# Key tiles fetched half by half, one half per step, in a windowed-attention and MoE kernel

## The chip, the cores and the metric

The kernel runs on one core of a Trainium2 chip. The metric is the device time of one execution in microseconds (us). The profile is one further execution, recorded by the hardware profiler. Engines are called as in the profile: PE (matrix multiplication) with PEld (its weight loads), DVE (vector), ACT (activations), POOL (GpSimd) and SP (a queue that issues transfers). POOL issues transfers too: all loads of this kernel's inputs after the first ones go through it[...].

## What is computed

Attention over a window of 32 tokens to both sides for 8 batches of 8 heads, 576 tokens each, head size 64, and on its output a two-layer network for 4608 tokens (512 to 2048 to 512):

```python
def _attn_ref(q, k, v):
    scores = scale * np.matmul(q, k.transpose(0, 1, 3, 2))
    mask = np.abs(pos[:, None] - pos[None, :]) <= 32
    scores = np.where(mask, scores, -1000000000.0)
    attn = np.exp(scores - np.max(scores, axis=-1, keepdims=True))
    attn = attn / (np.sum(attn, axis=-1, keepdims=True) + 1e-09)
    return np.matmul(attn, v)

def _moe_ref(x, w_in, w_out):
    h = x @ w_in
    g = h * (1.0 / (1.0 + np.exp(-1.702 * h)))
    return g @ w_out
```

The inputs q, k and v have the shape (8, 8, 576, 64); the output is (4608, 512) in float32.

## The kernel before

The 4608 tokens of all batches form one line. It is cut into 36 blocks of 128 tokens (index u, or m for V) and into tiles of 512 tokens (index i) for the loading of keys and queries. The whole order is written by hand: `head()` runs first, then `window(w)` for w = 4 to 19. Such a window is called a step here. Each engine works through its own instructions in the order in which the code names them, and waits where data or a buffer isn't ready.

A step w from 5 to 17 does three things at once. The attention of blocks a = 2w and b = 2w + 1 is computed: `scores`, `band` (the mask), `values`, `norm`. The first layer of the network runs for the pair of blocks of step w-1 (`layer1(w - 1, d)`, eight calls, list l1), the second layer for that of step w-2 (`product`, L394, with sums on DVE in `g_sums`, `keep` and `result`). PE therefore executes in a step: scores, products 1, 2, 5 and 6, the first call of layer1, the values, and then products and layer1 in turn.

The output of `norm`, x, must be transposed for layer1. From block 10 on a transfer does that: `x_T` (L315) issues a transposing transfer on SP for each block, xT<-x. Layer1 of the next step waits for both of the pair.

Keys and queries go through two stages. POOL loads them into a staging tile (ks and qs, three buffers each), and SP transposes them from there:

- `load_keys(i)` (L141 to L146) loads the keys of tile i in four chunks of 128 tokens, one transfer each, two where a chunk crosses from one batch to the next. `load_heads(i, "q")` (L138) loads the queries, in one or two transfers.
- `keys_X(i, c)` (L151) transposes chunk c into kT, a ring of 1536 tokens. `queries_X(i)` (L221) transposes a tile's queries into qT, after `pair_heads` has arranged them on DVE (qc<-qs).
- `load_v(m)` (L157) loads V for block m into one of 8 buffers; the transfer waits until `values` of block m-8 has read that buffer. `odd_v` copies V to a second layout.

Inside a step, the local function `loads()` (L606) issues V for blocks 2w + 6 and 2w + 7, then, in the even steps up to w = 10, the keys and queries of a whole tile, and in w = 4 those of two tiles. `loads()` stands at the front of the step, so on POOL the loads of a step follow directly on those of the step before; in w = 4 they stand behind two copies on POOL that wait for transposes of tile 3.

Towards the end of the step `feed(w)` (L727) prepares what later steps need: with i = (w + 4) // 2, an odd step pairs and transposes the queries of tile i and its key chunks 2 and 3, an even step transposes its chunks 0 and 1. SP takes these behind the xT transposes of the same step and ahead of those of the next.

Of the kernel before, what the change touches and what calls it, by code (L numbers as in the profile page):

```python
# [16 lines left out]
BF16 = mybir.dt.bfloat16  # L17
# [5 lines left out]
JT = 4  # L23
# [5 lines left out]
class _Kernel:  # L29
# [108 lines left out]
            self.nc.gpsimd.dma_start(self.stage[key][off // JT:(off + m) // JT, lo:hi, :],  # L138
                                     src[b, lo:hi, s:s + m, :].rearrange("h (p j) d -> p h (j d)", j=JT))

    def load_keys(self, i):  # L141

        kn = self.stage["k", i] = self.work.tile([128, JT, self.H, self.D], BF16, name="ks", tag="ks", bufs=3)
        for c in range(JT):
            for off, b, s, n in self.pieces(512 * i + 128 * c, 128):
                self.nc.gpsimd.dma_start(kn[off:off + n, c], self.k[b, :, s:s + n, :].rearrange("h s d -> s h d"))  # L146

# [447 lines left out]
    def window(self, w):  # L595
        nc, dve, sp = self.nc, self.nc.vector, self.nc.sync
        a, b = 2 * w, 2 * w + 1
        att = w < self.NW
        t, act = w - 2, nc.scalar
        l1 = [(lambda d=d: self.layer1(w - 1, d)) for d in range(8)] if w <= self.NW else []  # L600

        def run(lst, n=1):
            for _ in range(min(n, len(lst))):
                lst.pop(0)()

        def loads():  # L606
            for m in (2 * w + 6, 2 * w + 7):
                if m < self.NU:
                    self.load_v(m)
            for i in ((4, 5) if w == 4 else (w // 2 + 3,) if w % 2 == 0 else ()):  # L610
                if 512 * i < self.N:
                    self.load_keys(i)
                    self.load_heads(i, "q")

        if w == 4:
            l2 = [(lambda u=u, i=i: self.layer2(u, i, "oh"[u % 2], (dve, act)[u % 2])) for u in (4, 5) for i in range(4)]
            self.scores(7)
            self.scores(a)
            run(l2, 3)
            self.band(7)  # L620
            self.scores(b)
            run(l2)
            self.band(a)
            self.values(7, "th")
            self.gelu_table()
            for hp in range(4):
                self.pair_heads("q", 3, hp, act)
            self.queries_X(3)
            self.nc.gpsimd.tensor_copy(self.kT[:, :, RING:], self.kT[:, :, 0:64])
            self.nc.gpsimd.tensor_copy(self.qT[:, :, RP:RP + 8], self.qT[:, :, 0:8])  # L630
            loads()
            self.band(b)
            self.norm(7)
            run(l2, 2)
            self.values(a)
            self.values(b)
            run(l2)
            self.x_T(7, "t", nc.scalar)
            self.norm(a)
            self.x_T(a)  # L640
            self.norm(b)
            self.x_T(b)
            run(l2)
            for m in (10, 11):
                self.odd_v(m, dve)
            run(l1, 8)
            self.g_sums(w - 1, 0)
            self.feed(w)
            return
        loads()  # L650
        if not att:
            self.close(w, l1)
            return
        self.scores(a)
        if w > 5:
            self.scores(b)
        self.g_sums(t, 1, (0, 1))
        self.product(t, 1, "o")
        self.keep(t, 1, dve)
        self.product(t, 2, "h")  # L660
        if w == 5:
            self.scores(b)
        self.g_sums(t, 1, (2, 3))
        self.result(t, 11)
        self.gelu_table()
        self.product(t, 5, "t")
        self.band(a)
        self.product(t, 6)
        self.band(b, 0)
        self.keep(t, 6, dve)  # L670
        self.band(b, 1)
        run(l1)
        self.values(a)
        self.values(b)
        self.norm(a)
        self.x_T(a)
        self.product(t, 7)
        self.keep(t, 7, dve)
        self.result(t, 22)
        run(l1, 1)  # L680
        self.product(t, 4)
        self.result(t, 21, act)
        self.norm(b)
        self.x_T(b)
        self.product(t, 3)
        self.result(t, 12)
        run(l1, len(l1) - 4)
        self.g_sums(w - 1, 0)
        self.feed(w)
        run(l1, 4)  # L690
# [109 lines left out]
```

## Time and profile before

| what | value |
| --- | --- |
| median of 11 runs | 304.66 us |
| lowest, highest | 301.29 us, 309.97 us |
| the profiled execution | 310.95 us |
| its span, first to last instruction | 309.2 us |
| mean granted TensorE clock | 0.971 |
| data moved | 38.81 MB in 126026 packets |
| POOL's transfer queue (q0) | 79008 packets, 18.16 MB |
| SP's transfer queue (q1) | 46528 packets, 19.67 MB |

The profiled execution is slower than most of the runs. The rows of the profile name an operation by its line, its engine and "output<-input", a count, its busy time, the mean duration of one, and after the second bar the idle time of its engine just ahead of it with what ended that time. In the slices each digit is the busy share of one fortieth of the span (7.73 us), in tenths. A transfer has two times: that of its issue on the engine that owns the queue, and that from the start of the issue to its landing. xT<-x takes 2.4 us to landing at least, 4.2 in the median and 11.6 at most; ks<-in_k_dram 2.4, 8.1 and 21.7 us.

### The profile page before, as it was taken

To read this page: it belongs to the slowest core of one execution; us is meant where nothing else is said; L and a number is where in the kernel's file an instruction comes from. 1 tells how busy PE (TensorE), PEld (TensorE's weight loads), DVE (VectorE), ACT (ScalarE), POOL (GpSimd) and SP (SyncE) were. 2 spreads that over 40 slices of the span, in tenths; PEclk is the share of its full clock that TensorE was granted. 3 is DMA by queue.
4 is the path that set the end of the run, shared out by engine and by line. 5 is a ranking of instruction groups with operands and counts; after the bars stand their busy time and mean duration, and the time that the engine had idled before them with its cause. 6 is when DMAs were issued, how large, how long until landed. Compare 5 with 4: busy or idle time off the path is not lost.

```text
span 309.2 us, 9525 instructions
## 1 busy us (share of the span) xinstructions
PE 292.0 (94%) x4020; PEld 237.9 (77%) x4020; DVE 192.1 (62%) x571; ACT 187.6 (61%) x310; POOL 89.9 (29%) x132
## 2 busy tenths in 40 slices
PE   7889999999998499999589999999999999999995
PEld 3468765857886388888458888888888888888884
DVE  3653557776658148696535857776685858684353
ACT  4675457797848039485716766758584849485330
POOL 8784517830784322352043202020200000000000
PEclk9979999999999689999959999999999999999999
DMA  9999996999999999999989994895755030303012
GB/s 144 159 206 204 194 190 127 173 144 159 126 155 146 165 130 175 123 178 141 145 103 157 181 178 36 118 135 125 89 115 125 19 105 0 105 4 102 2 68 68
DMA packets 126026, 38.81 MB, mean 126 GB/s; under 512 B 104481, under 2 KB 121633, under 8 KB 125985
## 3 DMA queue, kind: packets, MB, share of 16 engines
q0 software_dynamic: 79008, 18.16, 72.6%
q1 hardware_dynamic: 46528, 19.67, 36.7%
q8 instruction: 31, 0.51, 0.7%
q10 hardware_dynamic: 448, 0.39, 0.5%
q14 instruction: 11, 0.08, 0.1%
HBM read 36.96 MB, written 9.44 MB: 150 GB/s over the span
## 4 chain that ended last, share of the span: by engine, by line
PE 84%; DMA 10%; POOL 2%; DVE 1%; ACT 1%; issue 0%; POOLq 0%; DVEq 0%
PE h_ps L332 40%; PE o_ps L394 28%; DMA xT<-x 7%; PE o_ps L344 7%; PE pv L292 4%; PE sc L263 3%; DMA qs<-in_q_dram 3%; PE tp L176 1%; POOL ve L157 1%; PE tp L319 0%; ACT g L334 0%; POOL ks L138 0%; DVE qc L106 0%; DVE o_sb L412 0%; POOL neg L237 0%
## 5 line engine op out<-in xcount | busy, mean ns | idle before, releaser
L332 PE MATMUL h_ps<-xT,w_in_sb 128*128 128x256 bf16 x1152 | 138.8, 277 | 10.3 <-DMA xT<-x 10.3
L334 ACT ACTIVATE g<-h_ps 128x512 f16<-128x512 f32 x144 | 85.7, 596 | 90.0 <-PE h_ps L332 88.7
L332 PEld LDWEIGHTS <-w_in_sb 128*128 128x128 bf16 x1152 | 113.7, 99 | 25.9 <-issue 5.8
L157 POOL DMA_DIRECT2D ve<-in_v_dram x40 | 34.0, 854 | 88.4 <-PE pv L292 68.3
L394 PEld LDWEIGHTS <-gs 128*128 128x128 f16 x480 | 46.5, 99 | 6.5
L394 PE MATMUL o_ps<-w_sum,gs 128*128 128x256 f16 x360 | 46.0, 279 | 0.0
L269 ACT ACTIVATE p<-sc 128x512 bf16<-128x512 f32 x72 | 37.2, 604 | 2.8 <-PE sc L263 2.6
L394 PEld LDWEIGHTS <-g 128*128 128x128 f16 x360 | 34.1, 98 | 4.5 <-ACT g L334 0.2
L371 DVE TENSOR_TENSOR gs<-g 128x512 f16<-128x512 f16 x30 | 12.7, 422 | 35.7 <-ACT g L334 35.7
L304 DVE TENSOR_TENSOR x<-pv,rec 128x256 bf16<-128x256 f32 x72 | 30.5, 424 | 2.5
L394 PE MATMUL o_ps<-w_out_sb,g 128*128 128x256 f16 x240 | 29.0, 273 | 0.0
L106 DVE COPY part<-o_ps 128x256 f32<-128x256 f32 x45 | 19.0, 423 | 14.1 <-PE o_ps L394 12.9
L303 DVE RECIPROCAL rec<-pv 128x4 f32<-128x4 f32 x72 | 12.5, 174 | 23.8 <-PE pv L292 23.8
L412 DVE TENSOR_TENSOR o_sb<-o_ps,part 128x256 f32<-128x256 f32 x45 | 19.0, 422 | 13.1 <-PE o_ps L394 12.5
L146 POOL DMA_DIRECT2D ks<-in_k_dram x27 | 22.7, 871 | 10.1 <-DMA qs<-in_q_dram 3.7
L281 DVE TENSOR_TENSOR p<-p,mask 128x512 bf16<-128x512 bf16 x64 | 24.8, 423 | 1.3 <-ACT p L269 1.1
L344 PE MATMUL o_ps<-w_out_sb,g 128*128 128x512 f16 x96 | 23.2, 380 | 0.0
L106 DVE COPY vo<-ve 64x528 bf16<-64x528 bf16 x65 | 21.1, 325 | 1.9 <-DMA ve<-in_v_dram 0.4
L431 ACT ACT_TABLE_LOAD x15 | 19.2, 1283 | 0.3
L269 ACT ACT_TABLE_LOAD x15 | 19.2, 1283 | 0.3
L292 PEld LDWEIGHTS <-p 128*64 128x64 bf16 x576 | 12.1, 117 | 6.8 <-DVE p L281 2.5
L394 PE MATMUL o_ps<-w_out_sb,gs 128*128 128x256 f16 x120 | 15.6, 273 | 0.0
(72 smaller groups left out, 247.3 us busy)
## 6 DMA issues: line engine op xcount, KB each, us to landing
out_dram<-o_sb SPq DMA_DIRECT2D x34, 256.0 KB, 3.1
ve<-in_v_dram POOLq DMA_DIRECT2D x32, 128.0 KB, 6.2
ks<-in_k_dram POOLq DMA_DIRECT2D x22, 128.0 KB, 8.2
w_in_sb<-in_moe_w_in_dram POOLq DMA_DIRECT2D x4, 512.0 KB, 11.5
w_out_sb<-in_moe_w_out_dram POOLq DMA_DIRECT2D x4, 512.0 KB, 12.1
qs<-in_q_dram POOLq DMA_DIRECT2D x2, 448.0 KB, 14.2
qs<-in_q_dram POOLq DMA_DIRECT2D x3, 256.0 KB, 7.7
qs<-in_q_dram POOLq DMA_DIRECT2D x2, 384.0 KB, 14.9
```

The costliest lines, as they stand in the source:

```text
L106: (eng.copy if eng is self.nc.scalar else eng.tensor_copy)(out, in_)
L146: self.nc.gpsimd.dma_start(kn[off:off + n, c], self.k[b, :, s:s + n, :].rearrange("h s d -> s h d"))
L157: self.nc.gpsimd.dma_start(self.ve[m % NV][off:off + n, :, :self.D], self.v[b, :, s:s + n, :].rearrange("h s d -> s h d"))
L269: nc.scalar.activation(p[:, eo].rearrange("k h (s j) -> k h s j", j=JT), sc[eo].rearrange("k h (j s) -> k h s j", j=JT), AF.Exp, scale=sel ...
L281: self.nc.vector.tensor_mul(pv, pv, msk.to_broadcast([128, 4, 2, SQ]))
L292: nc.tensor.matmul(acc[half][blk * 64:blk * 64 + 64, hh, :], p[:, h % 2, h // 2 * 2 + blk, :], vt[:, h, :D + 1], start=(hh == 0), stop=(hh ...
L304: nc.vector.tensor_mul(x[:, hs, :], acc[half][:, :, :D], rec[:, hs, :].to_broadcast([128, 4, D]))
L332: nc.tensor.matmul(hps[:, i, :], self.w_in_sb[:, kr, ff * 128:(ff + 1) * 128], self.xT[t][:, kr, :], start=(i == 0 and kr == 0), stop=(i = ...
L334: nc.scalar.activation(self.g[t][:, ffs[0]:ffs[1] + 1:ffs[1] - ffs[0], :], hps, AF.Gelu_apprx_sigmoid)
L344: nc.tensor.matmul(o_ps, self.g[t][:, ff, s * 128:(s + 1) * 128], self.w_out_sb[:, ff, :], start=(ff == 0), stop=(ff == self.NFF - 1))
L394: nc.tensor.matmul(self.part[t, key], x, y, start=(first and k == 0), stop=(k == 7), skip_group_check=True)
L431: self.nc.scalar.activation(self.spark, self.spark, AF.Gelu_apprx_sigmoid)
```

## The change

The keys of a tile after the fourth are no longer loaded at once. In an odd step w the first two chunks of tile (w + 5) // 2 are loaded, in the following even step the last two and the tile's queries. Tile 4 is loaded whole in w = 4, as before. Tile 5, which was loaded in w = 4 as well, is loaded in w = 5 and 6; tile 6 in 7 and 8 where it was in 6; tile 7 in 9 and 10 where it was in 8; tile 8 in 11 and 12 where it was in 10. `load_keys` takes a list of chunks and makes the staging tile at its first call for a tile. Nothing else is touched: V still comes first in each step, and `feed` keeps its order.

```diff
-    def load_keys(self, i):
-
-        kn = self.stage["k", i] = self.work.tile([128, JT, self.H, self.D], BF16, name="ks", tag="ks", bufs=3)
-        for c in range(JT):
+    def load_keys(self, i, chunks=range(JT)):
+
+        if ("k", i) not in self.stage:
+            self.stage["k", i] = self.work.tile([128, JT, self.H, self.D], BF16, name="ks", tag="ks", bufs=3)
+        kn = self.stage["k", i]
+        for c in chunks:
             for off, b, s, n in self.pieces(512 * i + 128 * c, 128):
                 self.nc.gpsimd.dma_start(kn[off:off + n, c], self.k[b, :, s:s + n, :].rearrange("h s d -> s h d"))
...
-            for i in ((4, 5) if w == 4 else (w // 2 + 3,) if w % 2 == 0 else ()):
-                if 512 * i < self.N:
-                    self.load_keys(i)
+            i = (w + 5) // 2
+            if 512 * i < self.N:
+                self.load_keys(i, range(4) if w == 4 else (0, 1) if w % 2 else (2, 3))
+                if w % 2 == 0:
                     self.load_heads(i, "q")
```

## The prediction

> **What bounds the kernel now.** The page first, its share table, the slices and the costliest group.
>
> ```profile
> PE 292.0 (94%) x4020; PEld 237.9 (77%) x4020; DVE 192.1 (62%) x571; ACT 187.6 (61%) x310; POOL 89.9 (29%) x132
> PEclk9979999999999689999959999999999999999999
> DMA  9999996999999999999989994895755030303012
> L332 PE MATMUL h_ps<-xT,w_in_sb 128*128 128x256 bf16 x1152 | 138.8, 277 | 10.3 <-DMA xT<-x 10.3
> ```
>
> TensorE is the bound, and all it loses after the head is 10.3 us of waiting for transposed activations (xT). The DMA engines are full until about 160 us and nearly idle after 190. Busy time step by step (a step is one window(w); from 80 us they are w = 5, 6, 7, 8, 9, 10) shows the price:
>
> ```profile
> 80.00:94.60 14.60, 14.60 (x216) 12.69 (x216) 9.97 (x29) 9.87 (x16) 12.45 (x16) 1.00 1.71 144
> 94.60:117.76 23.16, 17.63 (x226) 14.22 (x228) 11.32 (x36) 9.98 (x16) 8.60 (x11) 0.85 1.80 148
> 117.76:132.37 14.61, 14.61 (x225) 12.79 (x228) 10.43 (x30) 9.87 (x16) 4.90 (x7) 1.00 2.00 150
> 132.37:147.00 14.63, 14.63 (x221) 12.79 (x222) 11.38 (x36) 9.87 (x16) 5.34 (x7) 1.00 1.71 160
> 147.00:169.10 22.10, 17.34 (x224) 14.10 (x227) 10.17 (x32) 9.98 (x16) 6.13 (x7) 0.85 1.44 136
> 169.10:183.70 14.60, 14.60 (x221) 12.77 (x224) 10.90 (x36) 9.87 (x16) 1.76 (x2) 1.00 1.33 189
> ```
>
> Columns: stretch, length, then busy us of PE, PEld, DVE, ACT, POOL, then the clock and the DMA share. A step is 14.6 us; w = 6 takes 8.56 more and w = 9 takes 7.50 more, together 16.06. The profiled execution (310.95 us, span 309.2) would be 310.95 - 16.06 = 294.9 without them. The median of the runs, 304.66, is 9.8 above that and the runs 6.4 to 15.1: stalls of varying size explain the spread. Next SP's timeline, the loaded step w = 8 and the unloaded w = 12, then POOL's:
>
> ```profile
> 134.00 5.72 SPq L221 DMA_TRANSPOSE qT<-qc  x1
> 139.82 2.58 SPq L151 DMA_TRANSPOSE kT<-ks  x2
> 142.50 1.32 SPq L315 DMA_TRANSPOSE xT<-x  x1
> 144.59 2.80 SPq L315 DMA_TRANSPOSE xT<-x  x1
> ...
> 199.19 1.77 SPq L221 DMA_TRANSPOSE qT<-qc  x1
> 201.05 3.62 SPq L151 DMA_TRANSPOSE kT<-ks  x2
> 207.69 1.25 SPq L315 DMA_TRANSPOSE xT<-x  x1
> ```
>
> ```profile
> 86.31 4.08 POOL L146 DMA_DIRECT2D ks<-in_k_dram  x5
> 129.69 0.88 POOL L146 DMA_DIRECT2D ks<-in_k_dram  x1
> 142.18 0.88 POOL L157 DMA_DIRECT2D ve<-in_v_dram  x1 [2.09 <-PE o_ps L394]
> 158.83 1.75 POOL L157 DMA_DIRECT2D ve<-in_v_dram  x2 [15.78 <-PE pv L292]
> ```
>
> The chain of transposes in an even step (queries, two key chunks, two xT) runs from 134.0 to 156.0 (144.59 plus 11.4 to landing) beside the loads, 22.0 us; from 199.19 to 211.1 (207.69 + 3.4) without, 11.9. Its last xT must land 4.3 us into the next step. In w = 8 PE stood ready at 156.06 - 4.76 = 151.30. So the stall is the SP queue sharing the DMA engines with the POOL queue.
>
> **The change, part by part.**
>
> Nothing is removed: tiles 4 to 8 still take the same pieces at 871 ns of POOL each, and what POOL issues delays nobody (88.4 us of its idle time lie before V's loads alone). Only their times move, on POOL's queue alone; SP's order is unchanged. [...] POOL passes from one step's loads to the next as soon as V's buffers are free, which is after the values of w-1 (5.1 us into it), so a step's loads start in the step before.
>
> Pace of the load queue: issued from 79.75, the last V of step 9 lands at 142.18 + 16.9 = 159.1. In between 12 V pieces of 128 KB and four tiles of 1024 KB: 5632 KB in 79.3 us, 71 KB/us.
>
> *First stall (w = 6).* Up to step 6 the queue holds, before, V 14 to 19 and tiles 4 to 6 (3840 KB); after, 2816 KB. After, it runs to 79.75 + 39.7 = 119.4. The xT pair of step 5 is issued at 90.8 and 92.9 and lands at 104.5. So the queue is not empty there in either kernel. [...] The row: the late xT of w = 5 (92.89) and of w = 8 (144.59) took 11.6 and 11.4 us, though loads of 2900 KB were still to come at the first (3840 less 13.1 us of 71 KB/us) and 1030 KB at the second (14.5 us to 159.1). [...] Then the depth of POOL's queue is indifferent, only that it isn't empty: the first stall stays at 8.56. Were delay in proportion to depth, taking tile 5's 1024 KB from behind tile 4 would end it too, and the sum would be some 8.5 lower. [...]
>
> *Second stall (w = 9).* After, steps 4 to 9 put 1536 KB of V, tiles 4 to 6 and half the keys of 7 (3328 KB) on the queue: 4864 KB. Gates: step 7's loads are free at 106.5, 8's at 123.6, 9's at 137.5; the queue reaches them at 119.4, 126.6, 141.0, so it never starves and ends at 148.2, not 159.1. The chain from 134.0 then has 14.2 us at the slow pace (14.2/22.0 = 65%) and the other 35% at 11.9, 4.2 us: landing 152.4 against 151.3. Stall 1.1 us instead of 4.76. By the clock: after idle of 5.53 and 4.76 us the trace lost another 3.03 and 2.74 us at half clock. [...] for whole stalls the trace's 2.74 is used. Gain of the second stall 7.50 - 1.1 = 6.4 (ends: 0 if the chain isn't faster at all, 7.5).
>
> *New load in steps 10 to 12.* Before, w = 10's chain met only V of step 11. After: start of w = 10 at 162.7, chain from 164.3; step 10's loads (free at 153.2, 1024 KB) last to 167.6, step 11's (512 KB) from 167.8 to 175.0. So 10.5 us at slow pace (48%), 0.2 free (2%), the rest 6.0: 181.0 against 181.6. It just fits; I charge 0, ends 0 and 7.4 (whole 22.0 us: 4.7 late plus 2.7 clock). Odd steps 9 and 11 get the load that w = 7 has now: xT landed there at 127.12 + 8.3 = 135.4 against 136.6. Fits by 1.2.
>
> *Covers of the shorter lead.* V 16 to 19 no longer queue behind tile 5 and land earlier. The staging buffers (three) don't bind: the first half of tile 7, issued from 137.5, overwrites tile 4, whose last transposes were issued by 108.2. The first half of tile 6 lands by 126.6 and is transposed at the end of w = 8 (148.6); its queries by 141.0 and are paired at the end of w = 9 (about 158). 17 us at least. Were this gone, DVE would wait in pair_heads with band and norm behind it, and SP in the key transposes with xT behind them. If keys_X of the first half waited for the whole tile 5 (119.4), SP would stand from 114.7 to 119.4; the next xT is only due at 124.4: nothing. Late next after all this: the first stall.
>
> Sum on the profiled execution: 310.95 - 6.4 = 304.5. The median has only 9.8 us of stalls. Shared as in the profile (7.50 of 16.06), 4.6 of these are the second stall; 0.8 of it stays (1.1 scaled down, and less where there is no clock loss): 304.66 - 3.8 = 300.9, say 301.0.
>
> **The rivals.**
>
> *No gain.* The median run may carry the first stall whole (8.6) and 1.2 of the second; or the chain's pace is set by SP's own waits. For: nine of 11 runs lie at 304.3 or above, four of them within 0.2 us of 304.5. Against: 301.3 and 302.8 show the first stall smaller too. Time 304.3.
>
> *Slower: the loads never drain.* After the change V, keys and queries bring 1024 + 512 KB per two steps (29.2 us), 53 KB/us against a pace of 71. Should the pace beside the transposes fall under 53, each even step to w = 10 has its chain at the whole 22.0 us: the second stall stays and w = 11 gets one of 7.4, some 4.6 on the median's scale. 304.66 + 4.6 = 309.3. For: the load now falls in each step on the very xT pair. Against: 71 was measured under just that contention.
>
> *Both stalls go.* If depth matters after all: 294.9 + 1 = 296.
>
> That the split doesn't take effect is excluded by the code; the load steps follow from w alone.
>
> **How the numbers follow.** Second stall mostly gone, 0.46, time 301.0, own range 299 to 304; no gain 0.22; slower 0.20; both gone 0.12. Within 1% (301.6 to 307.7, about what a measurement of this kernel can't tell from no change): a third of the first case (0.15) and nearly all of the second (0.20), 0.35. Faster 0.31 + 0.12 = 0.43; slower 0.20 + 0.02 = 0.22. Range 296.5 to 308.5: it leaves out half of the both-gone and half of the slower case.
>
> **What would show it.** Step w = 6 still near 23 us, w = 9 near 15.7, w = 10 to 12 at 14.6; POOL's last V of step 9 landing about 148; 10.3 us of waiting for xT falls to about 6.6. It is wrong if w = 6 shrinks (depth counts), if w = 9 keeps over 20 us, or if w = 11 has a new stall.

## The result: a gain of one to two per cent, the second stall gone

| | kernel before | changed kernel |
| --- | --- | --- |
| median | 306.55 us (47 runs, 300.65 to 312.92) | 300.95 us (12 runs, 298.80 to 304.50) |
| ratio, 95% interval | | 0.9911 (0.9874 to 0.9947) |
| profiled execution | 310.95 us, span 309.2 | 299.62 us, span 297.9 |

Two later series of the same kernel gave 0.9855 (0.9759 to 0.995) and 0.9895 (0.9859 to 0.9932). The medians of all runs differ by more (0.982, and 0.977 and 0.982 in the later series): the ratio is formed from the runs within 1.5% of each kernel's fastest, 15 of 47 before and 9 of 12 after, so it leaves out the executions of the kernel before that stalled most and shifts with the fastest run that a series happens to have.

The page of the changed kernel, the lines that answer to those shown above (line numbers are two or three higher behind `load_keys`):

```profile
PE 286.8 (96%) x4020; PEld 235.3 (79%) x4020; DVE 191.3 (64%) x571; ACT 187.3 (63%) x310; POOL 89.9 (30%) x132
PEclk9999999999999899999999999999999999999999
DMA  8999999999999999999999949992963030303012
L334 PE MATMUL h_ps<-xT,w_in_sb 128*128 128x256 bf16 x1152 | 135.9, 274 | 4.9 <-DMA xT<-x 4.8
```

The work is the same to the instruction. The wait for xT has fallen from 10.3 to 4.8 us, and one of the two dips of the clock behind the head is gone. Busy time by step, from w = 5; the columns are as before:

```profile
78.02:92.82 14.80, 14.80 (x218) 12.74 (x217) 10.07 (x30) 9.87 (x16) 13.46 (x17) 1.00 1.79 139
92.82:113.63 20.81, 16.04 (x218) 13.40 (x218) 10.95 (x35) 9.98 (x16) 5.84 (x8) 0.92 1.68 155
113.63:128.50 14.87, 14.78 (x217) 12.74 (x216) 10.14 (x32) 9.90 (x16) 5.35 (x7) 1.00 1.82 165
128.50:143.10 14.60, 14.60 (x217) 12.80 (x216) 10.84 (x35) 9.87 (x16) 3.51 (x4) 1.00 1.56 168
143.10:157.70 14.60, 14.60 (x217) 12.81 (x216) 10.13 (x31) 9.87 (x16) 5.34 (x7) 1.00 1.27 129
157.70:172.30 14.60, 14.60 (x217) 12.81 (x216) 10.91 (x37) 9.87 (x16) 3.54 (x4) 1.00 1.64 181
172.30:186.90 14.60, 14.60 (x218) 12.81 (x216) 10.26 (x31) 9.87 (x16) 4.89 (x6) 1.00 0.95 107
```

Step 6 (second row) still loses 6.2 us. Step 9 (fifth row), which lost 7.5, runs at full pace, and so do 10 and 11 with their new load. Why step 9 is free is seen in SP's and POOL's timelines around step 8:

```profile
129.43 5.27 SPq L223 DMA_TRANSPOSE qT<-qc  x1
134.81 2.60 SPq L153 DMA_TRANSPOSE kT<-ks  x2
137.52 1.28 SPq L317 DMA_TRANSPOSE xT<-x  x1
...
139.55 1.22 SPq L317 DMA_TRANSPOSE xT<-x  x1
```

```profile
119.77 2.25 POOL L159 DMA_DIRECT2D ve<-in_v_dram  x3 [10.53 <-PE pv L294]
121.99 1.78 POOL L148 DMA_DIRECT2D ks<-in_k_dram  x2
123.73 1.40 POOL L138 DMA_DIRECT2D qs<-in_q_dram  x2
134.39 1.79 POOL L159 DMA_DIRECT2D ve<-in_v_dram  x2 [9.27 <-PE pv L294]
```

POOL issues the loads of step 8 in one go; before, up to 2.8 us lay between two of them. The second query piece, issued at 124.50, takes 10.5 us to landing, so all of them are through at 135.0; the next loads are issued at 134.39. Around this time the load queue (q0) has next to nothing to move. Its packets from 133 to 136 us, with their MB and their share of the DMA engines:

```profile
q0 software_dynamic: 15, 0.01, 1.8%
```

The last xT, issued at 139.55, lands 6.3 us later, at 145.9. Before it took 11.4 us. PE wants it at 147.4.

### The profile page after: what moved, and what is told of

The parts are those of the page before. It is cut to its first block, busy times and chain, and to the rows that moved or that the text cites. A ratio compares the mean times of both kernels' runs of the same rounds, so it can differ in the third digit from the quotient of the medians.

```text
span 297.9 us, 9525 instructions
## 1 busy us (share of the span) xinstructions
PE 286.8 (96%) x4020; PEld 235.3 (79%) x4020; DVE 191.3 (64%) x571; ACT 187.3 (63%) x310; POOL 89.9 (30%) x132
## 4 chain that ended last, share of the span: by engine, by line
PE 89%; DMA 5%; DVE 3%; ACT 1%; issue 0%; SPq 0%; DVEq 0%
PE h_ps L334 42%; PE o_ps L396 30%; PE o_ps L346 7%; PE pv L294 4%; PE sc L265 4%; DMA xT<-x 3%; PE tp L178 2%; DMA k_raw<-in_k_dram 1%; DVE vo L106 1%; PE tp L321 1%; DVE x L306 1%; DVE kT L106 1%; PE sc L247 0%; DVE o_sb L414 0%; DVE kc L106 0%
## 5 line engine op out<-in xcount | busy, mean ns | idle before, releaser
L334 PE MATMUL h_ps<-xT,w_in_sb 128*128 128x256 bf16 x1152 | 135.9, 274 | 4.9 <-DMA xT<-x 4.8
L334 PEld LDWEIGHTS <-w_in_sb 128*128 128x128 bf16 x1152 | 112.3, 98 | 19.0 <-issue 5.4
L396 PEld LDWEIGHTS <-gs 128*128 128x128 f16 x480 | 45.8, 98 | 5.8
L396 PE MATMUL o_ps<-w_sum,gs 128*128 128x256 f16 x360 | 44.4, 273 | 0.0
L106 DVE COPY part<-o_ps 128x256 f32<-128x256 f32 x45 | 19.1, 424 | 12.6 <-PE o_ps L396 11.4
L305 DVE RECIPROCAL rec<-pv 128x4 f32<-128x4 f32 x72 | 12.5, 174 | 16.2 <-PE pv L294 16.2
L294 PEld LDWEIGHTS <-p 128*64 128x64 bf16 x576 | 11.5, 113 | 6.2 <-DVE p L283 3.4
L396 PE MATMUL o_ps<-w_sum,g 128*128 128x256 f16 x120 | 15.5, 273 | 0.0
```

Of the source, the lines that this page charges most:

```text
L106: (eng.copy if eng is self.nc.scalar else eng.tensor_copy)(out, in_)
L294: nc.tensor.matmul(acc[half][blk * 64:blk * 64 + 64, hh, :], p[:, h % 2, h // 2 * 2 + blk, :], vt[:, h, :D + 1], start=(hh == 0), stop=(hh ...
L334: nc.tensor.matmul(hps[:, i, :], self.w_in_sb[:, kr, ff * 128:(ff + 1) * 128], self.xT[t][:, kr, :], start=(i == 0 and kr == 0), stop=(i = ...
L396: nc.tensor.matmul(self.part[t, key], x, y, start=(first and k == 0), stop=(k == 7), skip_group_check=True)
```

## The experiments

Each comparison is with the kernel before on the same chip; chips differ, so ratios and not medians are set side by side. One profile of each kernel shows where its loss sits. This table gives, for each profiled execution, how much each step is longer than 14.6 us, measured from its first scores to those of the next step:

| kernel | 5 | 6 | 7 | 9 | other | sum | ratio (95%) |
| --- | --- | --- | --- | --- | --- | --- | --- |
| before | 0.2 | 8.4 | 0 | 7.5 | 0.1 | 16.2 | 1 |
| before_again | 0.2 | 9.3 | 0 | 4.6 | | 14.1 | 0.9956 (0.9904 to 1.0008) |
| loads_first_whole | 13.7 | 0 | 0 | 0 | 0.1 | 13.8 | 0.9973 (0.9921 to 1.0025) |
| halves_early | 0.2 | 5.4 | 0.9 | 6.4 | | 12.9 | 1.0087 (1.0045 to 1.013) |
| later_tiles_only | 0.2 | 8.6 | 0 | 0 | 0.3 | 9.1 | 0.9859 (0.9815 to 0.9903) |
| tile5_only | 0.2 | 2.8 | 5.7 | 0 | | 8.7 | 0.9974 (0.9922 to 1.0026) |
| whole_later | 0.2 | 5.1 | 0.1 | 0 | | 5.4 | 0.9849 (0.9795 to 0.9904) |
| the change | 0.2 | 6.2 | 0.3 | 0 | | 6.7 | 0.9911 (0.9874 to 0.9947) |
| after_again | 0.2 | 4.1 | 1.1 | 0 | 0.1 | 5.5 | 0.9855 (0.9759 to 0.995) |
| after_c | 0.2 | 1.6 | 5.7 | 0 | 0.5 | 8.0 | 0.9895 (0.9859 to 0.9932) |
| loads_first | 5.5 | 0 | 0 | 0 | | 5.5 | 0.9768 (0.97 to 0.9836) |
| whole_later_first | 5.5 | 0 | 0.1 | 0.1 | | 5.7 | 0.9714 (0.9654 to 0.9774) |
| xT_on_pe | 1.9 | 0 | 6.6 | 0 | 0.4 | 8.9 | 0.9731 (0.9667 to 0.9794) |
| keys_first | 0.4 | 0.2 | 6.7 | 0 | | 7.3 | 0.9881 (0.9769 to 0.9993) |
| whole_later_keys_first | 1.8 | 0 | 6.6 | 0 | | 8.4 | 0.9848 (0.9756 to 0.9941) |
| pe_567 | 0.6 | 0.4 | 0.5 | 0 | 0.6 | 2.1 | 0.9727 (0.9635 to 0.9818) |
| pe_567_b | 0.6 | 0.5 | 0.4 | 0 | 0.1 | 1.6 | 0.9779 (0.971 to 0.9848) |
| pe_567_before | 0.6 | 0.5 | 0.9 | 0.9 | 0.2 | 3.1 | 0.9763 (0.9665 to 0.9861) |
| pe_567_before_b | 0.6 | 0.5 | 0.5 | 1.5 | | 3.1 | 0.9821 (0.975 to 0.9892) |
| pe_567_whole_later | 0.6 | 0.5 | 1.4 | 0 | 0.7 | 3.2 | 0.9726 (0.9633 to 0.982) |

### Which part of the change does it

`tile5_only` moves tile 5 and leaves 6 to 8 where they were:

```diff
-            i = (w + 5) // 2
-            if 512 * i < self.N:
-                self.load_keys(i, range(4) if w == 4 else (0, 1) if w % 2 else (2, 3))
-                if w % 2 == 0:
-                    self.load_heads(i, "q")
+            if w in (4, 5, 6):
+                i = (w + 5) // 2
+                self.load_keys(i, range(4) if w == 4 else (0, 1) if w % 2 else (2, 3))
+                if w % 2 == 0:
+                    self.load_heads(i, "q")
+            if w in (6, 8, 10):
+                self.load_keys(w // 2 + 3)
+                self.load_heads(w // 2 + 3, "q")
```

> Only tile 5 is taken out of step 4 (halves in steps 5 and 6); tiles 6, 7 and 8 are loaded whole in steps 6, 8 and 10 as in the kernel before. Theory (the gain is the load work of tiles 6 and 7 put off past the second stall): by step 6 the load queue holds the same 3840 KB as before, so step 6 stays near 21 to 23 us and step 9 near 22; ratio to the kernel before 0.997 to 1.003. Rival (the relief of the double load in step 4 is what counts): step 9 falls to 14.6 us and the ratio is that of the whole change, about 0.99.

`later_tiles_only` does the reverse:

```diff
+            if w == 4:
+                for i in (4, 5):
+                    self.load_keys(i)
+                    self.load_heads(i, "q")
             i = (w + 5) // 2
-            if 512 * i < self.N:
-                self.load_keys(i, range(4) if w == 4 else (0, 1) if w % 2 else (2, 3))
+            if w > 6 and 512 * i < self.N:
+                self.load_keys(i, (0, 1) if w % 2 else (2, 3))
```

> Tiles 4 and 5 are both loaded in step 4 as before; only tiles 6, 7 and 8 go in halves to steps 7 to 12. Theory: the load queue up to step 9 carries the same 4864 KB as in the changed kernel, so step 9 is at 14.6 to 16 us, step 6 at 20 to 23 us, ratio about 0.99, that of the whole change. Rival (relief in step 4 counts): step 9 stays near 22 us, ratio 1.00.

`whole_later` puts the tiles off without halving them:

```diff
-            i = (w + 5) // 2
-            if 512 * i < self.N:
-                self.load_keys(i, range(4) if w == 4 else (0, 1) if w % 2 else (2, 3))
-                if w % 2 == 0:
-                    self.load_heads(i, "q")
+            i = w // 2 + 2
+            if w % 2 == 0 and 512 * i < self.N:
+                self.load_keys(i)
+                self.load_heads(i, "q")
```

> Tiles 5 to 8 are loaded whole in steps 6, 8, 10 and 12: put off by one even step, but not halved. Theory (putting off counts, not halving): step 9 at 14.6 to 16 us, step 6 near 21, ratio about 0.99 as for the whole change; up to step 9 the load queue has 256 KB less than in it. Rival (an even load per step counts): the whole tile of an even step, 1280 KB or 18 us at 71 KB/us, falls on the xT pair of step 8 or 10 and a stall of 5 to 7.5 us comes back in step 9 or 11; ratio 1.00 or more.

`halves_early` halves them without putting them off:

```diff
-            i = (w + 5) // 2
+            i = 5 if w == 4 else (w + 7) // 2
+            if w == 4:
+                self.load_keys(4)
+                self.load_heads(4, "q")
```

> Keys in halves, but not put off: tile 5 stays in step 4, tile 6 is loaded in steps 5 and 6, tile 7 in 7 and 8, tile 8 in 9 and 10, so that the first half of each comes one step earlier than in the kernel before. Theory (putting off counts): the second stall stays, step 9 near 22 us, ratio 1.00 to 1.005. Rival (an even load per step counts): step 9 at 14.6 to 16 us, ratio about 0.99.

Putting off the tiles counts. Tile 5 alone brought nothing that the measurement can tell from no change; tiles 6 to 8 alone brought as much as the whole change; whole tiles put off brought as much as halves (297.3 us of span and steps 9 to 12 without a stall, so the even load per step is not needed); and halves that come earlier than in the kernel before made it slower by 0.9% (its one profile doesn't show where: the table has 12.9 us for it, less than for the kernel before). Steps 6 and 9 of `later_tiles_only`, which keeps the double load of step 4:

```profile
94.80:118.00 23.20, 17.51 (x219) 14.14 (x218) 11.21 (x35) 9.98 (x16) 6.06 (x7) 0.85 1.88 156
...
147.20:161.80 14.60, 14.60 (x217) 12.81 (x216) 10.11 (x31) 9.87 (x16) 5.34 (x7) 1.00 1.35 143
```

One expectation failed in a telling way. `tile5_only` should have stalled in steps 6 and 9. In its profile step 9 was free, and the second stall stood in step 7. Its steps 6 to 8:

```profile
95.00:112.40 17.40, 14.77 (x218) 12.71 (x218) 11.04 (x34) 9.98 (x16) 6.53 (x8) 1.00 1.66 153
112.40:132.70 20.30, 16.33 (x221) 13.69 (x221) 10.47 (x32) 9.98 (x16) 9.19 (x12) 0.92 1.85 172
132.70:147.30 14.60, 14.60 (x221) 12.78 (x220) 11.06 (x35) 9.87 (x16) 2.62 (x4) 1.00 1.91 178
```

This profiled execution took 303.77 us, its median 305.07, so a usual one loses some more than the 8.7 us of the table. But the stalls aren't tied to their steps.

### Can the stall that is left be removed?

The first stall looked like the work of one late transfer: POOL's two copies in step 4 wait for transposes while V and tile 4 stand behind them, SP then waits for tile 4's keys, 7.4 us in the changed kernel and 7.8 us before, and both xT of step 5 stand behind that. The wait in the kernel before:

```profile
SPq L151 <- DMA ks<-in_k_dram: 7.8, 1, 7.8
```

Three edits attack it. `loads_first` (and `loads_first_whole`, the same in the kernel before; `whole_later_first`, the same in `whole_later`):

```diff
+            loads()
             self.nc.gpsimd.tensor_copy(self.kT[:, :, RING:], self.kT[:, :, 0:64])
             self.nc.gpsimd.tensor_copy(self.qT[:, :, RP:RP + 8], self.qT[:, :, 0:8])
-            loads()
```

> The changed kernel, with the loads of step 4 issued on POOL ahead of its two copies of kT and qT, which wait until 70 and 78 us for transposes; POOL idles there, so V and tile 4 start near 64 instead of 78.5 and land near 83. Theory (first stall: SP stands 8 us for tile 4's keys with both xT of step 5 behind that wait, and these then share the DMA engines with the loads): SP's wait for the keys goes, the xT pair is issued some 4.7 us earlier, the idle 4.8 us of step 6 falls under 1; step 6 at 14.6 to 16 us, ratio to the kernel before 0.97 to 0.975. Rival (only the load queue being non-empty between 90 and 104 us counts, which it still is): step 6 stays near 20 us, ratio near 0.985 to 0.99.

> The kernel before, with the loads of step 4 (two tiles) issued ahead of the two copies on POOL. Theory: SP's wait for tile 4's keys goes and with it most of the first stall; the 2304 KB end 14 us earlier, so the load queue is through with step 9 near 145 instead of 159 us and the second stall shrinks too: ratio 0.97 to 0.985. Rival (the copies of kT and qT now wait behind 12 us of POOL's issuing, and scores of step 5 wait for them): step 5 longer by 2 to 6 us, ratio 0.99 to 1.01.

> Tiles 5 to 8 whole in steps 6, 8, 10, 12, and the loads of step 4 ahead of POOL's two copies. Theory: both stalls go, all steps from 5 at 14.6 to 15.5 us, ratio 0.965 to 0.975, the best of all. Rival: as for the changed kernel with the loads first; the whole tile in step 6 holds the queue full on the xT pair of step 5, step 6 near 19 us, ratio 0.985.

The wait for xT did go, but PE paid in step 5 instead. The waits of PE in `loads_first` between 78 and 125 us, and step 5:

```profile
PE sc L265 <- POOL qT L634: 3.4, 1, 3.4
```

```profile
78.40:98.40 20.00, 16.60 (x217) 13.70 (x216) 10.03 (x30) 10.09 (x16) 9.17 (x12) 0.91 1.71 167
```

The transpose of tile 3's queries, issued at 70.5, now ran beside the loads and took 13.4 us to landing where it takes 7.9 in the changed kernel; POOL's copy of its wrap and the scores of block 11 waited for it. With two tiles in front (`loads_first_whole`) that wait was 11.6 us and step 5 took 28.3; every other step ran at 14.6. The sum, 13.8, is nearly the 14.1 of the kernel before in its second profile. The ratios of `loads_first`, `whole_later_first` and of `xT_on_pe` below, 0.971 to 0.977, come from four runs each on one chip where the changed kernel wasn't run and where the kernel before was at 303.70 us at best (299.64 to 302.64 in the other series). They aren't set against 0.9911. That of `whole_later_first` lies where the theory expected it and that of `loads_first` just above; this doesn't save the theory, since step 5 took the loss.

`keys_first` sends only 256 KB ahead (`whole_later_keys_first` does so in `whole_later`):

```diff
+            self.load_keys(4, (0, 1))
             self.nc.gpsimd.tensor_copy(self.kT[:, :, RING:], self.kT[:, :, 0:64])
...
-                self.load_keys(i, range(4) if w == 4 else (0, 1) if w % 2 else (2, 3))
+                self.load_keys(i, (0, 1) if w % 2 else (2, 3))
```

> The changed kernel, with only the first two key chunks of tile 4 (256 KB) issued ahead of POOL's two copies in step 4; V, the other chunks and the queries stay behind them. Theory: SP's wait of 8 us for those keys goes, the xT pair of step 5 is issued 4 us earlier, and since the queue holds little while the query transpose is under way, POOL's copy of qT isn't late (loads_first lost 3.4 us there): step 5 at 14.6 to 15 us, step 6 at 14.6 to 17, ratio 0.965 to 0.975. Rival (arrears of the SP queue remain, since the load work between 78 and 104 us is less by only 256 KB): step 6 or 7 still longer by 4 to 6 us, ratio 0.98.

> The same two chunks first, with tiles 5 to 8 whole in steps 6, 8, 10 and 12. Theory: as keys_first and 0.5 to 1 us better, since step 5 carries only V: ratio 0.96 to 0.97, the best of all. Rival: no better than whole_later_first, 0.97 to 0.975.

`xT_on_pe` lets PE transpose the xT of step 5:

```diff
-        self.x_T(a)
+        self.x_T(a, "a" if w == 5 else None)
...
-        self.x_T(b)
+        self.x_T(b, "a" if w == 5 else None)
```

> The changed kernel, but the xT of step 5 is made by transposes on PE and a copy on DVE, for that step alone. Theory: step 6 loses its wait for xT, 14.6 to 15 us, step 5 gains 0.5 us of PE; if the SP queue has no other arrears, ratio 0.975 to 0.98. Rival (the SP queue is behind by as much, and the next xT pair is then late instead): step 7 longer by 3 to 6 us, ratio 0.985 to 0.99.

The profiles show what both rivals said; the ratio of `xT_on_pe`, 0.973, is better than its rival had it (0.985 to 0.99). Steps 5 to 7 of `keys_first`, then of `xT_on_pe`:

```profile
78.30:93.30 15.00, 14.96 (x217) 12.84 (x216) 10.04 (x30) 9.98 (x16) 11.25 (x14) 1.00 1.42 174
93.30:108.20 14.90, 14.85 (x221) 12.88 (x219) 11.10 (x35) 9.87 (x16) 6.43 (x8) 1.00 1.84 149
108.20:129.50 21.30, 17.12 (x221) 13.99 (x220) 10.16 (x32) 9.98 (x16) 5.35 (x7) 0.84 1.72 162
```

```profile
78.40:94.90 16.50, 15.67 (x226) 13.17 (x224) 10.90 (x31) 9.87 (x16) 13.82 (x17) 1.00 1.83 139
94.90:109.60 14.70, 14.70 (x222) 12.85 (x224) 11.35 (x36) 9.87 (x16) 4.87 (x6) 1.00 1.77 159
109.60:130.80 21.20, 16.36 (x221) 13.54 (x220) 10.11 (x32) 9.98 (x16) 5.36 (x7) 0.92 1.46 138
```

Step 6 is cured in both, and step 7 takes 21.3 and 21.2 us. Removing what releases the late xT moved the stall by one step and left the sum. In a second profile the kernel before and the changed kernel do the same on their own:

> The kernel before once more, for how its two stalls vary from one execution to the next. Assumption of the prediction: the second stall (step 9) is 47% of the stall time in any execution, in the profile 7.5 us. If so, this profile has step 9 longer than 14.6 us by some 45% of what steps 6 to 9 lose together. Rival: arrears of the SP queue are shared out anew each time, so the loss may sit in steps 6, 7 or 9 while its sum is what differs from the changed kernel. Ratio 0.995 to 1.005.

> The changed kernel once more on this chip, beside the next two. Step 6 (or 7) is longer by 5 to 9 us, step 9 at 14.6 us; ratio 0.98 to 0.99.

In `before_again` step 9 held 4.6 of the 13.9 us that steps 6 to 9 lost (33%, not 47%), and a later profile of the changed kernel (`after_c`) has the larger part of its loss in step 7 and not in step 6.

### One account or two stalls

The theory after this: what is late is not one transfer but the SP queue as a whole. Between about 78 us and step 9 the DMA engines have more to move than fits; PE pays when it needs an xT that stands at the end of that queue, in whichever step that is. That more is asked of the DMA engines than fits is read from their slices, nearly all at 9 until then; it isn't measured by itself. `pe_567` takes that need away for three steps, placing the PE transposes where the operands are ready (`pe_567_before` and `pe_567_whole_later` do the same to those kernels):

```diff
-        self.x_T(a)
+        by_pe = w in (5, 6, 7)
+        if not by_pe:
+            self.x_T(a)
...
         run(l1, 1)
+        if by_pe:
+            self.x_T(a, "a")
...
-        self.x_T(b)
+        if not by_pe:
+            self.x_T(b)
...
         run(l1, len(l1) - 4)
+        if by_pe:
+            self.x_T(b, "a")
```

> The changed kernel with the xT of steps 5, 6 and 7 made by PE transposes (placed where norm is done) and DVE copies. One account (arrears of the SP queue, worked off by step 8 with the load work put off): steps 5 to 7 at 15.0 to 15.8 us for the transposes, steps 6 to 9 without a wait for xT; sum of excess 1.5 to 3 us against 5.4 to 6.7 of the changed kernel, ratio 0.965 to 0.975. Rival (the arrears stay until somebody waits): 4 to 6 us in step 9, ratio 0.98 to 0.99.

> The kernel before, loads untouched, with the xT of steps 5, 6 and 7 made on PE as in pe_567. One account: more load work stands before step 9, so the arrears are not worked off and step 9 is longer by 5 to 10 us; ratio 0.98 to 0.995. Separate causes (first stall in step 6 gone, second as before or smaller by half): step 9 longer by 3 to 7.5 us, and the gain equals that of pe_567 over the changed kernel, 3 to 5 us.

> Tiles 5 to 8 whole in steps 6 to 12 and the xT of steps 5, 6 and 7 on PE. One account: as pe_567 or up to 1 us better, since the load queue has 256 KB less up to step 9; ratio 0.96 to 0.975. Rival: the whole tile of step 8 or 10 meets the xT pair there, step 9 or 11 longer by 2 to 5 us.

> pe_567 once more. One account: no wait for xT in any step, runs within 2% of each other, ratio 0.965 to 0.98 and 2 to 4 us below the changed kernel of the same call.

> pe_567_before once more. One account: in part of its runs a stall of 5 to 10 us in step 9 (runs at 305 to 309), the others within 2 us of pe_567; median 1 to 5 us above pe_567. Separate causes: the same as pe_567 within 1 us.

> The changed kernel on the same chip: ratio 0.98 to 0.992, steps 6 and 7 together longer by 5 to 7 us, step 9 at 14.6 us.

Steps 5 to 9 of `pe_567_b`: no wait for xT, and only the 0.4 to 0.6 us a step that the transposes add.

```profile
78.70:93.90 15.20, 15.20 (x225) 13.15 (x224) 11.12 (x32) 9.87 (x16) 12.14 (x15) 1.00 1.89 141
93.90:109.00 15.10, 15.10 (x229) 13.28 (x231) 11.79 (x37) 9.87 (x16) 5.77 (x7) 1.00 1.75 150
109.00:124.00 15.00, 15.00 (x225) 13.20 (x224) 11.13 (x34) 9.87 (x16) 5.37 (x7) 1.00 1.77 184
124.00:138.60 14.60, 14.60 (x217) 12.80 (x216) 10.73 (x34) 9.87 (x16) 3.52 (x4) 1.00 1.35 151
138.60:153.20 14.60, 14.60 (x217) 12.80 (x216) 10.14 (x31) 9.87 (x16) 5.34 (x7) 1.00 1.06 117
```

On one chip the medians were 296.02 us (`pe_567_b`), 297.79 (`pe_567_before_b`), 300.98 (`after_c`, the changed kernel) and 306.36 (before). `pe_567` beats both kernels: 0.9779 (0.971 to 0.9848) against 0.9895 (0.9859 to 0.9932). In the profile of `pe_567` SP's transposes were slow in these steps, and PE waited for no xT: two kT issued from 106.32 us took SP 5.88 us, two from 129.26 us took 2.52, so the queue had caught up by then. That slow transposes are harmless while nobody asks for an xT is thus shown for these steps. The SP queue also holds six xT fewer; how much of the gain comes from that isn't separated. What I expected of the kernel before was largely wrong: it paid 0.9 and 1.5 us in step 9, not 5 to 10. One run of four and two of six of `pe_567_before` lie 4.8 us or more above the rest, but so does one of six of `pe_567_b` (4.8), so the spread tells nothing. Beside PE transposes the change in the loads is worth 1.3 and 1.8 us by the medians, and the intervals overlap: not shown.

## Why the prediction was wrong: two stalls with a fixed price each

That the second stall would go was right. The step that failed is the sum: each stall had a price of its own, the first "stays at 8.56", and the median's 9.8 us of stalls were "shared as in the profile (7.50 of 16.06)", 4.6 us of them for the second stall, 3.8 of these gained. The runs show one loss that moves between steps 6, 7 and 9 from one execution to the next. Step 9 had 47% of it in the first profile of the kernel before and 33% in the second, and in three profiles of the changed kernel steps 6 and 7 lost 6.2 and 0.3, 4.1 and 1.1, 1.6 and 5.7 us. The gain was 2.7 us by the ratio and 5.6 by the medians.

- *What bounds the kernel*: right. In both kernels all that PE loses from step 5 on is the wait for xT and the lower clock after it; with that need removed in steps 6 to 8, both run at medians of 296 to 299 us.
- *Second stall*: right in kind, 0 left where 1.1 was predicted. The chain of step 8 took 16.4 us (129.43 to 145.9), between 22.0 and 11.9 and below the 18.4 forecast, because the load queue did starve. Step 8's loads were through at 135.0 (141.0 forecast), the last V of step 9 at 135.30 + 6.11 = 141.4 (148.2). Of these 6 to 7 us, 3.9 are that step 8 itself began earlier, at 128.50 and not at 132.37. The rest is the pace: 4864 KB from 78.53 to 141.4 are 77 KB/us, not 71.
- *First stall* "stays at 8.56": wrong, and by the prediction's own sign ("It is wrong if w = 6 shrinks"). In the profiled execution it was 6.2. Only 0.8 of the 2.2 us less are wait (5.53 to 4.77); the rest is that PE ran at half clock for 3.4 us after it and not for 6.8. Steps 6 and 7 together lost 5.2 to 8.5 us with tile 5 out of step 4 (five profiles: the change, `after_again`, `after_c`, `whole_later`, `tile5_only`) and 6.3 to 9.3 with it in (four: before, `before_again`, `later_tiles_only`, `halves_early`). These overlap, so by the stalls it is neither confirmed nor refuted that the depth of the other queue is indifferent; the prediction inferred it from two landing times of the kernel before, 11.6 and 11.4 us.
- *Steps 10 to 12* "just fits": right; step 10 and 11 at 14.6 in all three profiles, 0.5 us lost in step 12 in one. The shorter lead cost nothing.
- *Profiled sum* 304.5, measured 299.62. The 4.9 us: the head was 1.9 shorter (step 5 begins at 78.02, not 79.93), the first stall 2.2, the second 1.1, less 0.3 in step 7.
- *The median*: the term that was mis-sized. The ratio gives 2.7 us of 304.66 (1.6 to 3.8), the medians of the longer series, 306.55 and 300.95, give 5.6. The 11 runs that the forecast started from lay 1.9 us below the longer series. So that 301.0 was forecast and the median is 300.95 is luck: the start was 1.9 us too low and the gain 1.9 us too small. (A slip in the sum changes little: 1.1 scaled down is 0.7, not 0.8.)
- *Rivals*: no gain and slower are excluded by the interval; both gone didn't happen. The step that would have made it slower, a queue that never drains, is what `halves_early` comes nearest to, and it was slower.

How the two queues share the DMA engines is not shown by their packets either. In the kernel before, from 100 to 108 us, SP's queue (q1) and POOL's (q0) moved:

```profile
q1 hardware_dynamic: 2105, 0.90, 79.0%
q0 software_dynamic: 2110, 0.49, 70.9%
```

In the changed kernel they moved 2773 and 2815 packets from 98 to 106 us. From 93 to 104.5 us of the kernel before, nearly the flight of its late xT, the counts were 2414 and 3845: within 1.5% of each other in two windows, and far apart in the third.

Open: how the 5.5 to 8.0 us that the change leaves divide between loads, transposes and stores, and what decides in which step they fall.

## What to carry to other kernels

Where a queue is overcommitted for a stretch, add up the loss over all the steps of the stretch before naming a culprit: a stall that goes in one step and returns in the next has not been removed. Here, while the DMA slices stood at 9, loads issued two steps ahead of need went with late transfers that were needed sooner: the last xT of step 8 took 11.4 us to landing in the kernel before, and 6.3 with the tiles put off. In such a stretch put a load off, and halve it only if the burst itself collides. Or let another engine do the urgent transfer for the steps concerned.

## What the runs showed of the hardware

A wait of about 2.5 us can cost the clock or not. Step 6 of `after_again` and step 6 of `tile5_only`, PE's timeline:

```profile
99.70 1.86 PE L334 MATMUL h_ps<-xT,w_in_sb 128*128 128x256 bf16 x8 [2.51 <-DMA xT<-x]
```

```profile
101.96 1.03 PE L334 MATMUL h_ps<-xT,w_in_sb 128*128 128x256 bf16 x8 [2.63 <-DMA xT<-x]
```

After 2.51 us of waiting eight matmuls took 1.86 us and the step lost 4.1; after 2.63 us they took 1.03 and it lost 2.8. The granted clock tells why. In the kernel before its changes between 75 and 300 us lie at 103.57, 110.39, 154.77 and 161.59 us, which are 2, 13 and 2 times 3.41 us apart; in the changed kernel they lie at 101.47 and 104.88. Cut into stretches of 3.41 us, with each profile's changes on their edges, busy time (PE first) and clock (third number from the end) of `after_again` (two rows), `tile5_only` (two) and the kernel before (three):

```profile
96.14:99.55 3.41, 1.05 (x10) 0.69 (x8) 1.66 (x5) 2.28 (x4) 0.62 (x1) 1.00 1.55 139
99.55:102.97 3.42, 3.27 (x43) 2.30 (x44) 0.93 (x4) 0.60 (x1) 0.16 (x1) 0.50 1.75 141
97.77:101.18 3.41, 1.56 (x15) 1.15 (x12) 2.24 (x7) 2.79 (x5) 1.35 (x2) 1.00 1.52 175
101.18:104.59 3.41, 2.63 (x50) 2.23 (x51) 1.12 (x4) 0.60 (x1) 0.67 (x1) 1.00 1.55 162
103.57:106.98 3.41, 2.38 (x30) 1.64 (x32) 0.11 (x1) 0.48 (x1) 1.35 (x2) 0.50 1.61 142
106.98:110.39 3.41, 3.41 (x35) 2.47 (x30) 1.99 (x8) 0.12 (x1) 1.25 (x2) 0.50 1.88 146
110.39:113.81 3.42, 3.42 (x33) 3.07 (x32) 1.32 (x4) 1.35 (x3) 0.78 (x1) 1.00 1.85 105
```

PE's idle time in one stretch goes with the clock of the next. In `after_again` 2.36 us of the wait fell into one stretch, and the next had half clock; in `tile5_only` the wait was split, at most 1.85 us in one, and the clock stayed full. From step 5 on this holds in all twenty profiles: at full clock, up to 1.86 us idle in a stretch left the clock full and 2.03 or more was followed by half (both in `after_c`); at half clock, 0.77 us or more was followed by another stretch at half (`halves_early`) and 0.46 or less by full clock (the change). Beyond a wait for xT itself, one stretch at half clock cost 1.4 to 1.8 us and two cost 2.4 to 3.0. The prediction charges no loss of clock to the 1.1 us that it leaves of the second stall; this was an estimate, and 1.1 lies below the 1.86 us that left the clock full.
